# Exponentials in pairs of scales, and negated sines taken from ScalarE instead of VectorE

## The chip, the core and the metric

The kernel runs on one core of a Trainium2 chip. The time is the device time of one execution in microseconds; several executions are given with their median. The profile is of one such execution. In its rows PE is TensorE's matmuls (PEld its weight loads), DVE is VectorE, ACT is ScalarE, POOL is GpSimd and SP is SyncE, which here only issues DMAs.

## What is computed

Two independent halves, whose results are concatenated: a sliding, dilated attention (A) and a long convolution with a state-space kernel (B). Only B's kernel generation is touched by the change:

```python
def _B_ref(u, A_re, A_im, B_re, B_im, C_re, C_im, log_dt, Dskip):
    ...
    dt = jnp.exp(log_dt)[:, None]
    A = A_re + 1j * A_im
    logdA = dt * A                                   # [640, 192]
    P = jnp.exp(logdA[:, :, None] * l[None, None, :])  # l = 0 .. 2047
    K = jnp.einsum("dn,dnl,dn->dl", Cc, P, dB).real
    ...
    y = (K convolved with u along the sequence)      # by FFT of length 4096
    return y + u * Dskip[None, None, :]

return jnp.concatenate([a, b], axis=-1)
```

For each of 640 channels the kernel K has 2048 taps, each a sum over 192 complex modes of exp(l * dt * A).

## The kernel before

The 640 channels are worked off in 5 chunks of 128, `c` = 0 to 4, and each chunk in two halves, `h` = 0 and 1. A tap index is split as l = a + 8 b + 64 j, with a and b from 0 to 7 and j from 0 to 31, so that exp(l x) is a product of three factors. Each factor is a real exponential times a cosine and a sine.

*The exponentials* (`exps_chunk`, L213 to L223). `alpha` is the real part of dt * A in float32, 192 values in each partition for a chunk. The table `R` holds, for each of the 192, 48 entries: a = 0..7, then 8 b, then 64 j with j = 16..31 followed by j = 15..0. The three entries with scale 0 are set to 1 by GpSimd (L217, L218), and each of the other 45 is one ScalarE ACTIVATE, Exp with its scale, over 192 elements (L222). `R` has two buffers, R0 and R1, for even and odd chunks.

*The sines* (`trig_half`, L226 to L257). TensorE forms the phases in PSUM (`ps_ph`, L247 and L250), and ScalarE takes their sine (L255) into two tables: `TA` for a and b, and `TX` for j. `TX` has three planes of 17 entries: plane 0 (cosine, entries 0 to 16), plane 1 (sine), and plane 2, the negated sine, entries 1 to 16. For a half there are four TA operations and four TX operations on ScalarE. `TX` has one buffer, so that the sines of a half wait until the X products of the half before have read it. Exp and Sin need different ACT tables, and a table load (ACT_TABLE_LOAD) stands wherever ScalarE goes from one to the other.

*The products* (`small_half`, L268 to L296, all on VectorE). P = R's a-entries times TA, Q = P times the coefficients `cT`, F from Q; G from R's b-entries times TA; then the negated sines (L286), and for each of two quarters X = R's j-entries times TX. P has one buffer. `y_form` (L305) makes three Y products for each quarter, and `kgen_unit` multiplies X and Y on TensorE (`ps_k`, L318 and L323) to give the taps `Ksb`.

*What surrounds them.* In the same loop the FFT runs: `fwd` (matmuls at L337 and L343, their copies out of PSUM to A at L338 and to Sg at L344, both on ScalarE), products with the spectrum (L358 on VectorE), and the first stage of the inverse (L374, copy Z at L375 on ScalarE). `times_d` makes UD on VectorE (L387). ScalarE also makes two copies of the coefficients ahead of each chunk's exponentials (L206, L207).

*The order.* The program builds its instructions in the order of the code, and a scheduler puts them into one fixed queue for each engine; each engine then works strictly in its own order and waits on semaphores. `tc.issue_after(ins)` makes what follows come after `ins` on its engine, and `tc.keep_in_program_order` keeps an instruction at its place. In chunk c the code order is: products of half 0, sines of half 1, units of half 0 with transforms in between, products of half 1, then the exponentials of chunk c+1 (L748 to L750, after the last sine of half 1) and the sines of its half 0 (L751), then the units of half 1. After the fifth chunk come the attention and the second stage of the inverse FFT, which the change does not touch.

Of the kernel before, what the change touches and what calls it, by code (L numbers as in the profile page):

```python
# [10 lines left out]
A = mybir.AluOpType  # L11
ACT = mybir.ActivationFunctionType
AX = mybir.AxisListType
bf16 = mybir.dt.bfloat16
f32 = mybir.dt.float32
# [4 lines left out]
PI_LO = 3.1415925  # L20
# [31 lines left out]
    return F1, F64  # L52


R_MULT = [float(a) for a in range(8)] + [8.0 * b for b in range(8)] + [64.0 * (16 + i) for i in range(16)] + [64.0 * (31 - i) for i in range(16, 32)]
L1_OF_ROW = [16 + i for i in range(16)] + [31 - i for i in range(16, 32)]


# [23 lines left out]
def inline(nc, arr, name):  # L82
    return nc.inline_tensor(np.ascontiguousarray(arr).astype(np.float32).astype(ml_dtypes.bfloat16), name=name).ap()
# [126 lines left out]
        engine.tensor_copy(out=co[:, :, 3], in_=co[:, :, 0])  # L210


def exps_chunk(tc, pools, B, c):  # L213
    nc = tc.nc
    R = pools["tab"].tile([128, 48, NE_R, 4], bf16, name="R", tag=f"R{c % 2}")
    src = B["alpha"][:, c].rearrange("p u (q f) -> p (u q) f", f=4)
    nc.gpsimd.memset(R[:, :, 0:16:8, :], 1.0)  # L217
    nc.gpsimd.memset(R[:, :, 47, :], 1.0)  # L218
    for e, m in enumerate(R_MULT):
        if m == 0.0:  # L220
            continue
        nc.scalar.activation(out=R[:, :, e, :], in_=src, func=ACT.Exp, scale=m)  # L222
    return R  # L223


def trig_half(tc, pools, B, c, h):  # L226

    nc = tc.nc
    MM = nc.tensor.matmul
    TA = pools["tab"].tile([128, 24, 32, 4], bf16, name="TA", tag=f"TA{h}")  # L230
    TX = pools["tab"].tile([128, 24, 3, 17, 4], bf16, name="TX", tag="TX")
    CF1, CF64 = B["CF1"], B["CF64"]
    for kind in range(2):
        for uu in range(2):
            u = 2 * h + uu
            L1, L64 = B["LP"][:, 0, u, c], B["LP"][:, 1, u, c]
            qs = slice(12 * uu, 12 * uu + 12)
            if kind == 0:
                both = CF64[:, 0:1].to_broadcast([128, 16, 32])
                pair = [(TA, 0, 8, [(L1, CF1[:, 0:16]), (L64, both)]), (TA, 16, 8, [(L1, CF1[:, 16:32])])]  # L240
            else:
                pair = [(TX, 0, 9, [(L64, CF64[:, 1:19])]), (TX, 18, 8, [(L64, CF64[:, 19:35])])]
            pss = [pools["psum"].tile([128, 2, 512], f32, name="ps_ph", tag="bank2") for _ in pair]
            halves = [(ps[:, bk, 0:n * UW].rearrange("p (e w) -> p e w", w=UW), L, C[:, bk * n:bk * n + n, :], i == 0, i == len(ops) - 1)
                      for ps, (dst, e0, n, ops) in zip(pss, pair) for bk in range(2) for i, (L, C) in enumerate(ops)]
            for (o, L, rhs, first, last) in halves:
                MM(o[:, :, 0:32], lhsT=L[:, 0:128], rhs=rhs, start=first, stop=last, skip_group_check=True)  # L247
            for (o, L, rhs, first, last) in halves:
                for hh in range(2):
                    MM(o[64 * hh:64 * hh + 64, :, 32:48], lhsT=L[:, 128:192], rhs=rhs[:, :, 16 * hh:16 * hh + 16], start=False, stop=last,  # L250
                       skip_group_check=True, tile_position=(0, 64 * hh))
            for ps, (dst, e0, n, ops) in zip(pss, pair):
                words = ps[:].bitcast(mybir.dt.int16).rearrange("p b (w s) -> p b w s", s=2)[:, :, 0:n * UW, 0]
                dst = dst.rearrange("p q w e f -> p q (w e) f") if dst is TX else dst
                last = nc.scalar.activation(out=dst[:, qs, e0:e0 + 2 * n, :].rearrange("p q (b e) f -> p b e q f", b=2),  # L255
                                     in_=words.rearrange("p b (e q f) -> p b e q f", q=12, f=4), func=ACT.Sin, scale=PI_LO / 32768.0)
    return TA, TX, last  # L257


def bc(ap, axis, n):  # L260
    s = list(ap.shape)
    return ap.unsqueeze(axis).to_broadcast(s[:axis] + [n] + s[axis:])


def small_half(tc, pools, co, R4, TA, TX, h):

    nc = tc.nc
    V = nc.vector  # L268
    tab = pools["tabb"]
    R = R4[:, 24 * h:24 * h + 24]  # L270
    TT = lambda o, a, b, op: V.tensor_tensor(out=o, in0=a, in1=b, op=op)  # L271
    P = tab.tile([128, 24, 2, 8, 4], bf16, name="P", tag="P")
    F = tab.tile([128, 3, 24, 8, 4], bf16, name="F", tag="F")
    G = tab.tile([128, 4, 24, 8, 4], bf16, name="G", tag="G")
    TT(P[:], bc(R[:, :, 0:8, :], 2, 2), TA[:, :, 0:16, :].rearrange("p q (r a) f -> p q r a f", r=2), A.mult)
    Q = tab.tile([128, 24, 4, 8, 4], bf16, name="Q", tag="Y", bufs=4)
    co = co[:, 24 * h:24 * h + 24].rearrange("p q (s r) f -> p q s r f", r=2)
    TT(Q[:].rearrange("p q (s r) a f -> p q s r a f", r=2), bc(P[:], 2, 2), bc(co, 4, 8), A.mult)
    Qv = Q[:].rearrange("p q (s r) a f -> p r s q (a f)", r=2)
    TT(F[:, 1:3].rearrange("p s q a f -> p s q (a f)"), Qv[:, 0], Qv[:, 1], A.add)  # L280
    TT(F[:, 0], F[:, 1], F[:, 2], A.add)
    RB = R[:, :, 8:16, :].rearrange("p q a f -> p q (a f)")
    TT(G[:, 0:4:3].rearrange("p w q a f -> p w q (a f)"), bc(RB, 1, 2), TA[:, :, 16:32, :].rearrange("p q (w a) f -> p w q (a f)", w=2), A.mult)
    TT(G[:, 1], G[:, 3], G[:, 0], A.subtract)
    TT(G[:, 2], G[:, 3], G[:, 0], A.add)
    V.tensor_scalar(out=TX[:, :, 2, 1:17, :], in0=TX[:, :, 1, 1:17, :], scalar1=-1.0, scalar2=None, op0=A.mult)  # L286
    Xs = []
    for uu in range(2):
        qs = slice(12 * uu, 12 * uu + 12)
        X = tab.tile([128, 12, 3, 32, 4], bf16, name="X", tag="X", bufs=2)  # L290
        RX = R[:, qs, 16:48, :]
        TT(X[:, :, 0:2, 0:16, :], bc(RX[:, :, 0:16, :], 2, 2), TX[:, qs, 0:2, 0:16, :], A.mult)
        TT(X[:, :, 0:2, 16:32, :], bc(RX[:, :, 16:32, :], 2, 2), TX[:, qs, 0:3:2, 1:17, :], A.mult)
        TT(X[:, :, 2], X[:, :, 1], X[:, :, 0], A.subtract)
        Xs.append(X)
    return F, G, Xs  # L296
# [365 lines left out]
def body(tc, ctx, pools, prm, B_u, B_Dskip, Sd, Zd, UDd, A_x, A_wqkv, A_wo, out_a, out_b):  # L662
    nc = tc.nc
# [12 lines left out]
    R, trig = {}, {}  # L676
    with tc.tile_pool(name="prep_b", bufs=1) as pb, tc.tile_pool(name="prep_c", bufs=1) as pc, tc.tile_pool(name="prep_a", bufs=1) as pa, tc.tile_pool(name="psum_p", bufs=2, space=bass.MemoryType.PSUM) as psp:
        pools.update(prep_a=pa, prep_b=pb, prep_c=pc)
        B, fill = partB_prep(tc, dict(pools, psum=psp), prm)
        fill(0, 1, lambda u: None)  # L680
        Dn = pa.tile([128, 160], bf16, name="Dn")
        dsrc = B_Dskip.rearrange("(g ch) -> g ch", g=4)
        late = tc.keep_in_program_order
        late(nc.sync.dma_start(out=BD[:].rearrange("p a b n -> p (a b n)"), in_=inline(nc, cn["BD"], "c_BD")))
        late(nc.sync.dma_start(out=EA[:].rearrange("p a n -> p (a n)"), in_=inline(nc, cn["EA"], "c_EA")))
        late(nc.sync.dma_start(out=T2[:].rearrange("p a n -> p (a n)"), in_=inline(nc, cn["T2"], "c_T2")))
        for g in range(4):
            late(nc.sync.dma_start(out=Dn[32 * g:32 * g + 32, :], in_=dsrc[g].partition_broadcast(32)))
        coefficients(nc.gpsimd, B, 0)
        R[0] = exps_chunk(tc, pools, B, 0)  # L690
        trig[0, 0] = trig_half(tc, pools, B, 0, 0)
        usrc = B_u[0].rearrange("(l1 l0) (g ch) -> g l1 l0 ch", l0=64, g=4)
        fill(1, NCH, lambda g: late(nc.sync.dma_start(out=U[32 * g:32 * g + 32], in_=usrc[g])))
        nc.gpsimd.tensor_copy(out=Dsb[:], in_=Dn[:].rearrange("p (ut c) -> p c ut", c=NCH))
# [24 lines left out]
    for c in range(NCH):  # L719
# [6 lines left out]
        if c > 0:  # L726
            P1, P2, last = products(tc, pools, Sk[c - 1], Sd[c - 1], fp, True)
# [15 lines left out]
        with ExitStack() as order:  # L743
            if c > 0:
                order.enter_context(tc.issue_after(last.ins))
            F, G, Xs = small_half(tc, pools, B["cT"][:, c], R[c], *trig[c, 1][:2], 1)
        if c < LAST:
            with tc.issue_after(trig[c, 1][2].ins):  # L748
                coefficients(nc.scalar, B, c + 1)
                R[c + 1] = exps_chunk(tc, pools, B, c + 1)  # L750
            trig[c + 1, 0] = trig_half(tc, pools, B, c + 1, 0)  # L751
        else:
            att.open_q0()
# [54 lines left out]
    def fill(some, n=1):  # L808
        for f in some[0:n]:
            f()  # L810
        del some[0:n]
# [14 lines left out]
    for i0, ni, j0, nj, done in ((0, 128, 2, 3, 0), (128, 128, 2, 3, 1), (256, 128, 0, 4, None), (256, 256, 4, 1, 2), (384, 128, 0, 4, 3)):  # L826
        for w in range(W):
            att.av_step(i0, ni, j0, nj, w)
            if (done, w) in LOADS:
                qr, c = LOADS[done, w]  # L830
# [78 lines left out]
```

## Time and profile before

| | us |
|---|---|
| median of 3 executions | 439.51 |
| lowest and highest | 439.4, 442.8 |
| the profiled execution | 438.98 |
| its span, first to last instruction | 437.2 |

| group (line, engine, operation, shapes) | times | busy us | mean ns |
|---|---|---|---|
| L305 VectorE, Y, 128x3072 bf16 | 60 | 102.9 | 1751 |
| L222 ScalarE, Exp into R, 128x192 from float32 | 225 | 59.3 | 358 |
| L338 ScalarE, copy A, 128x1024 | 40 | 37.6 | 1036 |
| L344 ScalarE, copy Sg, 128x1024 | 40 | 37.6 | 1027 |
| L271 VectorE, X, 128x1536 bf16 | 40 | 36.4 | 951 |
| L255 ScalarE, Sin into TA, 128x768 | 40 | 30.6 | 822 |
| L255 ScalarE, Sin into TX, 128x864 | 20 | 18.1 | 907 |
| L255 ScalarE, Sin into TX, 128x768 | 20 | 16.5 | 826 |
| L286 VectorE, negated sines, 128x1536 bf16 | 10 | 5.5 | 554 |
| ACT_TABLE_LOAD at L222 and L255 | 9 | 11.5 | 1283 |

"Mean" is the duration of one operation from its recorded start to its end. Operations of one engine that follow each other directly overlap in the records by some 0.08 to 0.1 us, so the step from start to start is shorter than the mean, and the busy time, in which overlaps count once, is less than the count times the mean. Five chunks of 45 exponentials make the 225 at L222. A timeline row gives start, length, engine, line, operation, what it writes and reads with shapes, how many were merged into the row, and in brackets how long the engine had been idle before it and what ended that.

### The profile page before, as it was taken

Reading aid. Unit: us, or ns where it says so; the run is one execution under the profiler, and the core shown is the slowest. Engines: PE = TensorE matmul, PEld = TensorE weight load, DVE = VectorE, ACT = ScalarE, POOL = GpSimd, SP = SyncE. Lnnn points to the kernel's source line nnn. Section 1 sums busy time; section 2 is a strip of 40 time slices with the busy share of each in tenths; the row PEclk is TensorE's granted clock in tenths of the full one; section 3 lists DMA queues with packets and bytes.
Section 4 is the critical chain, followed back from the end, with each engine's and each line's share of the span. In section 5 each row is a group of like instructions: output and inputs, shape, how many; then the busy total and the mean of one; then the engine's idle time right before and its main releaser. Section 6 shows DMA issues by size and latency. Waiting matters only on the chain.

```text
span 437.2 us, 17687 instructions
## 1 busy us (share of the span) xinstructions
PE 358.4 (82%) x8041; PEld 241.1 (55%) x8041; DVE 391.3 (89%) x386; ACT 314.0 (72%) x570; POOL 44.5 (10%) x85
## 2 busy tenths in 40 slices
PE   1397659989886998879778799999899897399995
PEld 0145546866863677556665665545555674134443
DVE  7889999999997999999999989946978989999751
ACT  3974998889999899979997845342858344544663
POOL 7440000000000000000010000400001204102110
PEclk9996577999999898889999899999999999659999
DMA  5569102163233402324079933500210907957343
GB/s 143 186 141 200 18 3 109 39 227 94 99 123 123 97 28 98 144 103 99 27 258 241 236 75 135 178 0 3 67 32 1 265 17 201 228 141 225 96 107 114
DMA packets 45131, 51.62 MB, mean 118 GB/s; under 512 B 31376, under 2 KB 38992, under 8 KB 42368
## 3 DMA queue, kind: packets, MB, share of 16 engines
q1 hardware_dynamic: 41520, 41.41, 35.4%
q0 software_dynamic: 3392, 8.95, 7.0%
q8 instruction: 63, 1.03, 1.0%
q10 hardware_dynamic: 144, 0.12, 0.1%
q14 instruction: 12, 0.10, 0.1%
HBM read 28.03 MB, written 18.35 MB: 106 GB/s over the span
## 4 chain that ended last, share of the span: by engine, by line
PE 49%; ACT 29%; DVE 14%; issue 5%; DMA 1%; SPq 1%; DVEq 0%; ACTq 0%
ACT R L222 10%; ACT A L338 6%; PE ps_k L318 6%; PE ps_ph L247 6%; PE ps_k L323 6%; PE ps_op L420 6%; PE ps_k L470 4%; PE ps_q L488 4%; PE ps_ph L250 4%; ACT Sg L344 4%; PE ps_f L343 4%; PE ps_v L501 2%; DVE prod L521 2%; ACT Z L375 2%; PE ps_o L420 2%
## 5 line engine op out<-in xcount | busy, mean ns | idle before, releaser
L305 DVE TENSOR_TENSOR Y<-F,G 128x3072 bf16<-128x3072 bf16 x60 | 102.9, 1751 | 0.6 <-PE ps_k L323 0.6
L222 ACT ACTIVATE R<-LPC 128x192 bf16<-128x192 f32 x225 | 59.3, 358 | 0.1
L247 PE MATMUL ps_ph<-LPC 128*128 128x256 bf16 (+1 forms) x200 | 41.5, 311 | 17.3 <-DMA LPC<-lo 8.7
L318 PE MATMUL ps_k<-Y,X 128*32 128x64 bf16 x1920 | 47.2, 239 | 7.3 <-DVE Y L305 3.8
L323 PE MATMUL ps_k<-Y,X 64*32 64x64 bf16 x1920 | 43.8, 233 | 3.4 <-issue 3.3
L344 ACT CAST Sg<-ps_f 128x1024 bf16<-128x1024 f32 x40 | 37.6, 1027 | 7.3 <-PE ps_f L343 7.3
L318 PEld LDWEIGHTS <-X 128*32 128x32 bf16 x1920 | 32.1, 117 | 17.4 <-issue 9.0
L343 PE MATMUL ps_f<-A,T 128*128 128x128 bf16 x320 | 27.3, 259 | 14.9 <-ACT A L338 14.2
L338 ACT CAST A<-ps_f 128x1024 bf16<-128x1024 f32 x40 | 37.6, 1036 | 0.7 <-PE ps_f L337 0.6
L271 DVE TENSOR_TENSOR X<-R,TX 128x1536 bf16<-128x1536 bf16 x40 | 36.4, 951 | 0.0
L323 PEld LDWEIGHTS <-X 64*32 64x32 bf16 x1920 | 29.6, 113 | 12.1 <-issue 4.4
L255 ACT ACTIVATE TX<-ps_ph 128x864 bf16<-128x864 int16 (+1 forms) x40 | 31.9, 867 | 5.3 <-DVE X L271 2.5
L343 PEld LDWEIGHTS <-T 128*128 128x128 bf16 x320 | 25.6, 119 | 16.1 <-issue 14.9
L585 DVE TENSOR_TENSOR prod<-v,atp 128x2048 bf16<-128x2048 bf16 (+2 forms) x32 | 31.3, 1018 | 2.0 <-PE ps_o L420 1.8
L255 ACT ACTIVATE TA<-ps_ph 128x768 bf16<-128x768 int16 x40 | 30.6, 822 | 3.4 <-PE ps_ph L250 3.0
L250 PE MATMUL ps_ph<-LPC 128*64 128x128 bf16 (+1 forms) x400 | 29.6, 249 | 0.0
L247 PEld LDWEIGHTS <-LPC 128*128 128x128 bf16 x200 | 15.0, 102 | 25.9 <-issue 19.1
L420 PE MATMUL ps_op<-wo,o 128*128 128x320 bf16 x160 | 28.5, 315 | 0.8 <-ACT o L595 0.4
L358 DVE TENSOR_TENSOR P<-P,Sg 128x4096 bf16<-128x4096 bf16 x10 | 22.9, 2288 | 4.1 <-DMA P<-Sdram 3.2
L250 PEld LDWEIGHTS <-LPC 128*64 128x64 bf16 x400 | 15.2, 118 | 19.1 <-issue 18.9
L611 ACT CAST ob<-ps_op 128x320 bf16<-128x320 f32 x28 | 11.9, 431 | 19.0 <-PE ps_op L420 17.3
L337 PE MATMUL ps_f<-BD,U 128*64 128x128 bf16 x320 | 19.4, 285 | 6.1 <-ACT A L338 3.3
(129 smaller groups left out, 661.2 us busy)
## 6 DMA issues: line engine op xcount, KB each, us to landing
Sdram<-Sg SPq DMA_DIRECT2D x5, 1024.0 KB
P<-Sdram SPq DMA_DIRECT2D x5, 1024.0 KB
P<-Sdram SPq DMA_DIRECT2D x10, 512.0 KB
Zdram<-Z SPq DMA_DIRECT2D x5, 1024.0 KB
Z<-Zdram SPq DMA_DIRECT2D x30, 128.0 KB
U<-in_B_u_dram SPq DMA_DIRECT2D x4, 640.0 KB
UDdram<-UD SPq DMA_DIRECT2D x10, 256.0 KB
out_dram<-ysb SPq DMA_DIRECT2D x32, 80.0 KB
```

The costliest lines, as they stand in the source:

```text
L222: nc.scalar.activation(out=R[:, :, e, :], in_=src, func=ACT.Exp, scale=m)
L247: MM(o[:, :, 0:32], lhsT=L[:, 0:128], rhs=rhs, start=first, stop=last, skip_group_check=True)
L250: MM(o[64 * hh:64 * hh + 64, :, 32:48], lhsT=L[:, 128:192], rhs=rhs[:, :, 16 * hh:16 * hh + 16], start=False, stop=last, skip_group_check= ...
L255: last = nc.scalar.activation(out=dst[:, qs, e0:e0 + 2 * n, :].rearrange("p q (b e) f -> p b e q f", b=2), in_=words.rearrange("p b (e q f ...
L271: TT = lambda o, a, b, op: V.tensor_tensor(out=o, in0=a, in1=b, op=op)
L305: nc.vector.tensor_tensor(out=Y[:].rearrange("p q (b a) f -> p q b a f", a=8), in0=fa, in1=gb, op=A.mult)
L318: MM(ps[32 * g:32 * g + 32, t], lhsT=X[:, q, 2 - k, :, f], rhs=Ys[k][:, q, :, f], start=(t == 0 and k == 0), stop=False, tile_position=(0, ...
L323: MM(ps[32 * g:32 * g + 32, t], lhsT=X[hb, q, 2 - k, :, f], rhs=Ys[k][hb, q, :, f], start=False, stop=(k == 2), tile_position=(64 * (g // ...
L338: nc.scalar.copy(out=A1[:, :, 32 * b:32 * b + 32].rearrange("p k (j g) -> p k j g", g=4), in_=ps[:].rearrange("p j k g -> p k j g"))
L343: last = MM(ps[:, kk], lhsT=C["T2"][:, 8 * b + kk, :], rhs=A1[:, 8 * b + kk, :], start=(kk % 4 == 0), stop=True, skip_group_check=True)
L344: nc.scalar.copy(out=Sg[:, :, 8 * b:8 * b + 8, :], in_=ps[:].rearrange("p k (j g) -> p j k g", g=4))
L420: self.MM = lambda *a, **k: self.tc.keep_in_program_order(self.nc.tensor.matmul(*a, **k))
```

## The change

The scale-0 entries are still set by GpSimd. For the others, `exps_chunk` first makes a tile `twice` with two planes, 2 * alpha and alpha, in float32. Entries whose scales are m and 2 m are then written by one ACTIVATE on 384 elements, which reads both planes with scale m and writes both entries; entries that have no partner are written as before, from alpha. For the scales 1 to 7 these are the pairs (1, 2) and (3, 6) and the single entries 4, 5, 7; the same for 8 to 56; for 64 j there are 10 pairs and 11 single entries. In all there are 17 single operations and 14 pairs in a chunk, and the single ones come first in the code.

The two planes are made on VectorE for chunk 0, in a tile of their own, and on GpSimd for chunks 1 to 4, where `twice` takes the buffer of P (`tag="P"`).

In `trig_half` each PSUM tile with the sines of j is read by a second Sin with the negated scale, which writes plane 2 of TX; the VectorE operation at L286 goes.

```diff
-R_MULT = [float(a) for a in range(8)] + ...
...
-def exps_chunk(tc, pools, B, c):
+def exps_chunk(tc, pools, B, c, engine, twice):
     nc = tc.nc
     R = pools["tab"].tile([128, 48, NE_R, 4], bf16, name="R", tag=f"R{c % 2}")
-    src = B["alpha"][:, c].rearrange("p u (q f) -> p (u q) f", f=4)
+    alpha = B["alpha"][:, c].rearrange("p u w -> p (u w)")
+    for b in range(2):
+        engine.tensor_scalar(out=twice[:, b], in0=alpha, scalar1=2.0 - b, scalar2=None, op0=A.mult)
     nc.gpsimd.memset(R[:, :, 0:16:8, :], 1.0)
     nc.gpsimd.memset(R[:, :, 47, :], 1.0)
-    for e, m in enumerate(R_MULT):
-        if m == 0.0:
-            continue
-        nc.scalar.activation(out=R[:, :, e, :], in_=src, func=ACT.Exp, scale=m)
+    one, two = [], []
+    for places in ({a: a for a in range(1, 8)}, {8 * a: 8 + a for a in range(1, 8)}, {64 * j: j if j > 15 else 47 - j for j in range(1, 32)}):
+        left = sorted(places)
+        while left:
+            m = left.pop(0)
+            e, step = places[m], 0
+            if 2 * m in left:
+                left.remove(2 * m)
+                step = places[2 * m] - e
+            (two if step else one).append((m, e, step))
+    for m, e, step in one + two:
+        src = twice[:].rearrange("p b (q f) -> p q b f", f=4)
+        if step == 0:
+            src, out = alpha.rearrange("p (q f) -> p q f", f=4), R[:, :, e, :]
+        elif step < 0:
+            out = R[:, :, e + step:e + 1:-step, :]
+        else:
+            src, out = src[:, :, ::-1, :], R[:, :, e:e + step + 1:step, :]
+        nc.scalar.activation(out=out, in_=src, func=ACT.Exp, scale=float(m))
     return R
...
-                last = nc.scalar.activation(out=dst[:, qs, e0:e0 + 2 * n, :]..., func=ACT.Sin, scale=PI_LO / 32768.0)
+                for at, sign in ((e0, 1), (35, -1))[:2 if e0 == 18 else 1]:
+                    last = nc.scalar.activation(out=dst[:, qs, at:at + 2 * n, :]..., func=ACT.Sin, scale=sign * PI_LO / 32768.0)
...
-    V.tensor_scalar(out=TX[:, :, 2, 1:17, :], in0=TX[:, :, 1, 1:17, :], scalar1=-1.0, scalar2=None, op0=A.mult)
...
-        R[0] = exps_chunk(tc, pools, B, 0)
+        R[0] = exps_chunk(tc, pools, B, 0, nc.vector, pa.tile([128, 2, 192], f32, name="twice"))
...
         if c < LAST:
+            twice = pools["tabb"].tile([128, 2, 192], f32, name="twice", tag="P")
             with tc.issue_after(trig[c, 1][2].ins):
                 coefficients(nc.scalar, B, c + 1)
-                R[c + 1] = exps_chunk(tc, pools, B, c + 1)
+                R[c + 1] = exps_chunk(tc, pools, B, c + 1, nc.gpsimd, twice)
```

More of the change, by code (lines that the diff above doesn't have):

```diff
@@ L52, in table_consts_np @@
     return F1, F64
-R_MULT = [float(a) for a in range(8)] + [8.0 * b for b in range(8)] + [64.0 * (16 + i) for i in range(16)] + [64.0 * (31 - i) for i in range(16, 32)]
 L1_OF_ROW = [16 + i for i in range(16)] + [31 - i for i in range(16, 32)]
@@ L254, in trig_half @@
                 dst = dst.rearrange("p q w e f -> p q (w e) f") if dst is TX else dst
-                last = nc.scalar.activation(out=dst[:, qs, e0:e0 + 2 * n, :].rearrange("p q (b e) f -> p b e q f", b=2),
-                                     in_=words.rearrange("p b (e q f) -> p b e q f", q=12, f=4), func=ACT.Sin, scale=PI_LO / 32768.0)
+                for at, sign in ((e0, 1), (35, -1))[:2 if e0 == 18 else 1]:
+                    last = nc.scalar.activation(out=dst[:, qs, at:at + 2 * n, :].rearrange("p q (b e) f -> p b e q f", b=2),
+                                         in_=words.rearrange("p b (e q f) -> p b e q f", q=12, f=4), func=ACT.Sin, scale=sign * PI_LO / 32768.0)
     return TA, TX, last
```

## The prediction

> **What bounds the kernel now.** I read the page's busy times first, then the chain of waits, the timelines of the three engines that the edits touch, and a table of VectorE's busy time by stretch.
>
> ```profile
> PE 358.4 (82%) x8041; PEld 241.1 (55%) x8041; DVE 391.3 (89%) x386; ACT 314.0 (72%) x570; POOL 44.5 (10%) x85
> PE 49%; ACT 29%; DVE 14%; issue 5%; DMA 1%; SPq 1%; DVEq 0%; ACTq 0%
> ```
>
> VectorE (DVE in the rows) is busiest and ScalarE (ACT) takes 29% of the chain, but these are means over stages. The edits lie in the stage up to 285 us, so I asked for VectorE's busy time in four stretches of it (start:end, length, busy, operations): in each chunk from shortly before product P of half 1 to the same product of the next chunk's half 0.
>
> ```profile
> core 0: us, DVE busy (x), PEclk, DMA share, GB/s
> 54.00:76.00 22.00, 22.00 (x22) 0.77 0.11 45
> 106.00:133.00 27.00, 24.33 (x23) 0.94 0.29 105
> 160.00:184.00 24.00, 24.00 (x23) 0.91 0.29 113
> 211.00:234.00 23.00, 23.00 (x23) 0.93 0.60 194
> ```
>
> Three of the four have no idle time at all; each operation starts some 0.08 us before the one ahead of it ends. The idle 2.7 us of the second lie at its end:
>
> ```profile
> 131.04 3.16 ACT L255 ACTIVATE TA<-ps_ph 128x768 bf16<-128x768 int16 x4
> ...
> 133.35 0.96 DVE L271 TENSOR_TENSOR P<-R,TA 128x1536 bf16<-128x1536 bf16 x1 [3.02 <-ACT TA L255]
> ...
> 184.28 0.95 DVE L271 TENSOR_TENSOR P<-R,TA 128x1536 bf16<-128x1536 bf16 x1
> ```
>
> P(2,0), product P of chunk 2's half 0, waited 3.02 us for its sines. At 184.28 they had been there for about 1 us, at 233.99 for 0.7. VectorE sets the pace, and ScalarE's queue of exponentials, table load and sines comes in just ahead of it.
>
> **VectorE's side.** Ten negations go (TX at L286, 554 ns, 0.47 from start to start). Nine lie in the dense stretch: 9 x 0.47 = 4.2 us off it. The tenth, at 30.80, had itself waited 1.29 us for ScalarE.
>
> **ScalarE's sines.** Twenty are added, on 128x768. The four TA sines at 231.04 take 2.92 us: (2.92 - 0.81) / 3 = 0.70 each from start to start; the mean row of the TX sines, 826 ns, is the upper bound. I take 0.71, so 2.84 us a chunk.
>
> **ScalarE's exponentials.** The 45 of a chunk become 17 single ones and 14 pairs, the same elements in fewer starts. A single one costs 11.49 us / 45 = 0.255. A pair has 192 elements more; the 480- and 320-wide copies to ysb (563 and 429 ns) give 0.84 ns an element, so 0.255 + 0.16 = 0.415. That saves 0.09 a pair, 1.3 us a chunk. Bounds: nothing (two singles, 0.51) and 3.6 (a pair as dear as a single). Net, ScalarE gains 1.5 us of work a chunk. In the first chunk the 1.3 us are on the path: the sines wait for the exponentials that run from 9.79 to 21.30, while the first TA matmuls are done by 20.8. Two copies of alpha on VectorE there (0.17 each by the like row at L177) sit before a 1.69 us wait of VectorE and cost nothing; without that cover, 0.35.
>
> **The copies on GpSimd.** For chunks 1 to 4 GpSimd makes two copies of alpha, one doubled, into `twice`, which takes the buffer of P. They wait for Q(c,1), the last reader of P: done at 58.2, 109.8, 163.8 and 214.7. All 14 pairs of the next chunk wait for them, and ScalarE works in order: behind a waiting pair stand the remaining pairs, the table load, the TA sines of P(c+1,0), and whatever copies out of PSUM were put after it. On GpSimd's queue stand the memsets of R and later the loads of wkq, all with tens of us to spare. So the question is when GpSimd (POOL) gets to run. These are the rows of GpSimd operations that read SBUF beside VectorE, with VectorE's own:
>
> ```profile
> 25.15 1.80 POOL L209 TENSOR_SCALAR cT<-cT 128x192 bf16<-128x192 bf16 x1 [0.54 <-ACT cT L196]
> ...
> 279.80 3.98 POOL L481 COPY kT<-kT 128x280 bf16<-128x280 bf16 x1 [5.74 <-ACT kT L471]
> ```
>
> ```profile
> 25.44 0.95 DVE L191 TENSOR_TENSOR p<-p,p 128x768 f32<-128x768 f32 x1
> 26.42 1.18 DVE L193 TENSOR_SCALAR cn<-p,dtc 128x192 bf16<-128x192 f32 x4
> ...
> 276.74 6.75 DVE L305 TENSOR_TENSOR Y<-F,G 128x3072 bf16<-128x3072 bf16 x4
> 286.48 1.30 DVE L518 TENSOR_TENSOR prod<-ql,kT 128x1024 bf16<-128x1024 bf16 x2 [2.99 <-ACT ql L489]
> ```
>
> The kT copy starts at 279.80 and ends at 283.78. VectorE's run of Y products ends at 276.74 + 6.75 = 283.49: the copy ends 0.29 us after VectorE falls idle, having let two starts of a Y pass. The operation at L209 spans one start of a TENSOR_TENSOR and ends at 26.94, 0.55 us after the last of them (26.39). Another GpSimd copy of 192 elements, beside TENSOR_SCALARs, took 0.34. I read this as GpSimd shut out while VectorE runs TENSOR_TENSORs without a gap. From Q(c,1) to P(c+1,0) there is nothing else on VectorE once the negation is gone.
>
> The Trainium skill ("SBUF — State Buffer", Who interferes with whom) says that a VectorE operation with two SBUF inputs and a GpSimd operation that reads SBUF exclude each other, and that whoever issues first holds the ports for one whole instruction. By that, GpSimd waits out one VectorE operation, 1.75 us at most; the kT copy waited out three, and the row decides. The skill's "Perfetto Trace Analysis" (GPSIMD Engine Instruction) calls reported GpSimd spans unreliable, which is a reason for not being surer of this than I am.
>
> **The sum.** With GpSimd shut out, `twice` is written only when VectorE has nothing left to start, which is at P(c+1,0) itself. From there: two copies at 0.29 to 0.55, say 0.85 together; 14 pairs at 0.415, 5.8; table load 1.28; three sines, 2 x 0.71 + 0.81 = 2.2. That is 10.1 us of VectorE standing still in each of four chunks. It replaces waits of 0.57 (at 76.67, behind P(1,0)), 3.02, 0 and 0: 9.5 + 7.1 + 10.1 + 10.1 = 36.8. Off this go 4.2 for the negations, 1.3 at the start, and about 1 of the two waits at 250.4 and 255.3 (0.92 and 1.17), as TensorE and the loads have had time. Net +30.3. On the profiled execution, 438.98 us (span 437.2, the rest around it), that is 469.3; the median shown, 439.51, is 0.5 above it: **470 us**.
>
> Its own bounds: if a pair stands ahead of the four Sg copies, ScalarE has 3.7 us more to do after release (13.8 a chunk, about +45: 485). But TensorE then stops too for want of PSUM, and VectorE may run out of Y buffers and stop up to 4.6 us early, which lets GpSimd in sooner; with the Sg copies ahead that leaves 5.5 a chunk (+12: 452).
>
> **Rivals.**
>
> *GpSimd gets in promptly* (the other side). Then `twice` is there some 3 us after Q(c,1), while the 17 single exponentials still cover ScalarE for 4.3. The place that decides is the sines of P(c+1,0): ScalarE's period of 50.5 us (180.50 to 231.04) grows by 1.5, VectorE's of 49.7 (184.28 to 233.99) shrinks by 0.9, less two GpSimd copies that now block it. P(2,0) comes out +0.4 (two exponential batches at -1.3, three sets of added sines at +1.42, start -1.3); two chunks more add 3.0, of which some 2 us vanish in ScalarE's present waits (5 us in those 100) and 0.7 in the lead of the sines. The last half gives back 0.5: 438.98 + 0.2 + 0.5, about **440**. For it: two spans are thin evidence. Against: both rows say otherwise. The rule of the Trainium skill weighed above, taken by itself, gives this rival.
>
> *VectorE stays the bound and ScalarE keeps up*: -4.2 - 1.3 = -5.5, so **434**. For it: VectorE's dense stretch. Against: the sines' lead of under 1 us, and the copies' own time on the shared ports.
>
> *The copies out of PSUM queue behind the pairs as well*: Z (2.8 for three), A (3.7), a TensorE reply (1.1) and Sg (3.7) after release, 11.3 more, less the 4.6 that VectorE stops early: +6.7 in four chunks, **497**. For it: in the profile the exponentials stand ahead of A at 57 to 61. Against: from chunk 1 on most A and Z stand ahead of the last exponentials.
>
> That the change does not do what it says is no rival of weight: each pair is one ACTIVATE with 384 elements.
>
> **Chances and range.** GpSimd shut out with the order as now 0.63; the same with copies behind the pairs 0.11; prompt 0.19; VectorE bound 0.07. About 1%, 4.4 us, is what a measurement here can tell from no change. The first two are slower by more than that (0.74), the third within it (0.19), the fourth faster (0.07). The forecast's own range is 452 to 486; down to 438 it takes in the prompt rival and leaves out 0.07 below and 0.11 above.
>
> **What would show it.** Right: the GpSimd TENSOR_SCALARs on `twice` have long spans that end within 0.6 us of the end of a VectorE run; ScalarE idle before a pair, released by GpSimd; P(c+1,0) waiting 5 to 14 us for TA in four chunks; 384-wide exponentials near 0.41 from start to start. Wrong: those spans under 2 us, with VectorE's operations stretched instead; no ScalarE wait on GpSimd; then the time is near 440 and the sines' lead decides. If pairs cost 0.5 each, a chunk gains 1.3 us.

## The result, and the profile after

| | before | after |
|---|---|---|
| median of 6 executions, us | 440.19 | 492.37 |
| lowest and highest | 438.2, 442.8 | 486.1, 496.4 |
| the profiled execution, us | 438.98 | 486.13 |
| its span | 437.2 | 484.4 |

The changed kernel takes 1.1137 times as long, 95% interval 1.1053 to 1.122. Ratios here and below leave out executions that lie over 1.5% above the fastest of their kernel (here 495.8 and 496.4 us), while medians keep them. By the medians it is 52 us more, where 30 were forecast, and the median lies 6 us above the range.

From the page of the changed kernel, first the busy times, then the chain by engine, then three of its costliest groups (busy us and mean ns of one, then idle time ahead and what ended most of it):

```profile
PE 363.0 (75%) x8041; PEld 242.2 (50%) x8041; DVE 389.4 (80%) x378; ACT 321.6 (66%) x520; POOL 97.7 (20%) x93
...
PE 27%; DVE 8%; ACT 7%; issue 3%; ACTq 0%; DVEq 0%
...
L323 DVE TENSOR_TENSOR Y<-F,G 128x3072 bf16<-128x3072 bf16 x60 | 103.3, 1754 | 31.3 <-PE ps_k L341 31.3
L219 POOL TENSOR_SCALAR twice<-LPC 128x192 f32<-128x192 f32 x8 | 55.6, 6965 | 168.7 <-DVE Q L290 103.1
...
L240 ACT ACTIVATE R<-twice 128x384 bf16<-128x384 f32 x70 | 29.6, 516 | 37.5 <-POOL twice L219 37.5
```

No engine has much more work than before (VectorE even 2 us less); the span is longer because engines stand still. GpSimd (POOL) is the exception: its eight copies into `twice` show 55.6 us, 7.0 us each, and ScalarE waits 37.5 us for them. The chain is of less use here: its shares add up to 45% only, and GpSimd does not appear in it.

The table of VectorE's busy time (start:end, length, busy, operations), for the stretches that answer to the four shown of before:

```profile
core 0: us, DVE busy (x), PEclk, DMA share, GB/s
55.40:95.90 40.50, 21.65 (x21) 0.66 0.09 34
131.70:157.30 25.60, 24.63 (x23) 0.93 0.27 106
182.90:218.10 35.20, 24.45 (x24) 0.78 0.30 114
243.80:278.00 34.20, 23.22 (x22) 0.80 0.49 147
```

The three stretches that had no gap before now hold 18.9 us of idle time (chunk 0), 10.8 (chunk 2) and 11.0 (chunk 3); that of chunk 1, which had 2.7, holds only 1.0. GpSimd's timeline says why:

```profile
59.24 16.40 POOL L219 TENSOR_SCALAR twice<-LPC 128x192 f32<-128x192 f32 x2 [26.33 <-issue]
135.32 1.86 POOL L219 TENSOR_SCALAR twice<-LPC 128x192 f32<-128x192 f32 x2 [59.12 <-DVE Q L290]
186.69 20.98 POOL L219 TENSOR_SCALAR twice<-LPC 128x192 f32<-128x192 f32 x2 [43.96 <-DVE Q L290]
247.57 16.38 POOL L219 TENSOR_SCALAR twice<-LPC 128x192 f32<-128x192 f32 x2 [39.34 <-ACT R L240]
```

and VectorE's timeline at the end of the third:

```profile
205.16 1.30 DVE L405 TENSOR_TENSOR UD<-U,Dsb 128x1024 bf16<-128x1024 bf16 x1
217.22 0.96 DVE L290 TENSOR_TENSOR P<-R,TA 128x1536 bf16<-128x1536 bf16 x1 [10.75 <-ACT TA L274]
```

Of the 20.98 us, 20.32 are the first of the two copies (the longest in its group). It ends at 186.69 + 20.32 = 207.01, 0.55 us after VectorE's last operation ended at 206.46; the second takes the rest. The first copies of chunks 0 and 3 end 0.55 us after VectorE's run as well. Then ScalarE does the 14 pairs, the table load and the sines while VectorE stands at P(3,0) for 10.75 us.

Chunk 0 costs more, and ScalarE's timeline shows why:

```profile
75.68 5.89 ACT L240 ACTIVATE R<-twice 128x384 bf16<-128x384 f32 x14 [18.05 <-POOL twice L219]
81.47 3.72 ACT L356 CAST A<-ps_f 128x1024 bf16<-128x1024 f32 x4
86.29 3.76 ACT L362 CAST Sg<-ps_f 128x1024 bf16<-128x1024 f32 x4 [1.10 <-PE ps_f L361]
90.07 1.28 ACT L274 ACT_TABLE_LOAD   x1
91.36 2.23 ACT L274 ACTIVATE TA<-ps_ph 128x768 bf16<-128x768 int16 x3
```

with TensorE's timeline

```profile
82.51 1.19 PE L355 MATMUL ps_f<-BD,U 128*64 128x128 bf16 x16 [22.70 <-ACT A L356]
```

and VectorE's:

```profile
72.69 1.75 DVE L323 TENSOR_TENSOR Y<-F,G 128x3072 bf16<-128x3072 bf16 x1
93.28 1.76 DVE L323 TENSOR_TENSOR Y<-F,G 128x3072 bf16<-128x3072 bf16 x1 [18.85 <-PE ps_k L341]
```

Four copies A and four copies Sg stand behind the 14 pairs. TensorE waits 22.7 us for A to empty PSUM, with the taps' matmuls behind in its queue; these alone free the Y buffers, so VectorE runs out of buffers with Y products still to make. That stop lets the copies in, but ScalarE then has 15.7 us of its queue to work through (75.68 to 91.36) before the first sine.

By stretch, between the starts of the products P(c,0), in us of change against before. "Forecast" takes the terms of the sum in their places, with 0.47 off for each of the nine negations (one lies in the stretch from P(0,0), two in each later one); "second profile" is of run e8 below, the same kernel once more:

| stretch | forecast | after | second profile |
|---|---|---|---|
| start to P(0,0), at 33.87 before | -1.3 | +0.8 | +0.6 |
| P(0,0) to P(1,0), 41.9 before | +9.1 | +18.4 | +18.3 |
| P(1,0) to P(2,0), 57.6 | +6.1 | +3.8 | +12.6 |
| P(2,0) to P(3,0), 50.9 | +9.2 | +9.9 | +10.8 |
| P(3,0) to P(4,0), 49.7 | +9.2 | +10.2 | +10.3 |
| P(4,0) to the last Y, 49.5 | -1.9 | +2.7 | +3.0 |
| after that, 153.7 | 0 | +1.4 | +1.4 |
| sum | +30.4 | +47.2 | +57.0 |

The second profile lies 26.6 us above the forecast: 9.2 in the stretch from P(0,0), 6.5 in that from P(1,0), 4.9 in the last one before the attention, 6.0 in the others together. No cause was found for the 1.4 us behind the last Y.

### The profile page after: what moved, and what is told of

Same layout as the page of the kernel before. It is cut to its first block, busy times and chain, and to the rows that moved or that the text cites. A ratio compares the mean times of both kernels' runs of the same rounds, so it can differ in the third digit from the quotient of the medians.

```text
span 484.4 us, 17644 instructions
## 1 busy us (share of the span) xinstructions
PE 363.0 (75%) x8041; PEld 242.2 (50%) x8041; DVE 389.4 (80%) x378; ACT 321.6 (66%) x520; POOL 97.7 (20%) x93
## 5 line engine op out<-in xcount | busy, mean ns | idle before, releaser
L219 POOL TENSOR_SCALAR twice<-LPC 128x192 f32<-128x192 f32 x8 | 55.6, 6965 | 168.7 <-DVE Q L290 103.1
L265 PE MATMUL ps_ph<-LPC 128*128 128x256 bf16 (+1 forms) x200 | 43.0, 320 | 30.9 <-ACT TA L274 11.8
L240 ACT ACTIVATE R<-twice 128x384 bf16<-128x384 f32 x70 | 29.6, 516 | 37.5 <-POOL twice L219 37.5
L274 ACT ACTIVATE TX<-ps_ph 128x768 bf16<-128x768 int16 (+1 forms) x60 | 45.6, 862 | 8.2 <-DVE X L290 5.5
L355 PE MATMUL ps_f<-BD,U 128*64 128x128 bf16 x320 | 19.9, 280 | 23.6 <-ACT A L356 22.7
L341 PEld LDWEIGHTS <-X 64*32 64x32 bf16 x1920 | 29.8, 113 | 10.8 <-issue 2.7
L355 PEld LDWEIGHTS <-U 128*64 128x64 bf16 x320 | 19.1, 206 | 24.3 <-issue 23.5
L376 DVE TENSOR_TENSOR P<-P,Sg 128x4096 bf16<-128x4096 bf16 x10 | 22.8, 2285 | 8.6 <-DMA P<-Sdram 8.4
```

Of the source, the lines that this page charges most:

```text
L219: engine.tensor_scalar(out=twice[:, b], in0=alpha, scalar1=2.0 - b, scalar2=None, op0=A.mult)
L274: last = nc.scalar.activation(out=dst[:, qs, at:at + 2 * n, :].rearrange("p q (b e) f -> p b e q f", b=2), in_=words.rearrange("p b (e q f ...
L341: MM(ps[32 * g:32 * g + 32, t], lhsT=X[hb, q, 2 - k, :, f], rhs=Ys[k][hb, q, :, f], start=False, stop=(k == 2), tile_position=(64 * (g // ...
L355: MM(ps[64 * ri:64 * ri + 64, j], lhsT=src_fn(8 * b + j), rhs=C["BD"][:, wh, ri, :], start=(j % 4 == 0), stop=True, skip_group_check=True, ...
```

## The experiments

The theory, called ports theory in the expectations: GpSimd's copies are shut out by VectorE's two-input operations, and all else follows from ScalarE's fixed order behind the late pairs. The rivals: the copies are late because they wait for the buffer of P, whatever engine makes them (buffer theory); the added sines and the longer exponentials are too much for ScalarE (load theory); GpSimd itself is slow. Ratios are to the kernel before, run on the same chip beside each.

**e1, the copies on VectorE.**

```diff
-                R[c + 1] = exps_chunk(tc, pools, B, c + 1, nc.gpsimd, twice)
+                R[c + 1] = exps_chunk(tc, pools, B, c + 1, nc.vector, twice)
```

> The two copies of alpha of chunks 1 to 4 are made by VectorE in place of GpSimd; all else is the changed kernel. Ports theory (GpSimd's copies are shut out while VectorE runs two-input operations without a gap, and ScalarE stands in order behind the pairs that wait for them): the copies take 0.25 us each at their place in VectorE's queue, ScalarE waits under 1 us for them in each chunk, and the time falls from 492 to about 441 us (438 to 446). Buffer theory (the copies come late because they wait for the buffer of P, whatever engine makes them): ScalarE still waits 10 us or more in three chunks, 480 or more. Load theory (the added sines and the longer exponentials are what ScalarE can't fit in): 480 or more, with no wait on the copies.

452.03 us, ratio 1.0166 (1.0093 to 1.0239). With 0.26 us a copy, 9.7 of the 11.4 points are gone by this one word. The rest was not expected. ScalarE's timeline:

```profile
67.71 1.35 ACT L240 ACTIVATE R<-twice 128x384 bf16<-128x384 f32 x3 [9.31 <-DVE twice L219]
```

In chunk 0 the scheduler put the two copies at 66.38 and 67.42 in VectorE's queue, among the X products, so that ScalarE's queue stood for 9.3 us even so. That stretch is 8.3 us longer than before, P(1,0) to P(2,0) is 3.1 longer, and the start costs 1.6.

**e2, the second sines alone, in the kernel before.**

```diff
-                last = nc.scalar.activation(out=dst[:, qs, e0:e0 + 2 * n, :]..., func=ACT.Sin, scale=PI_LO / 32768.0)
+                for at, sign in ((e0, 1), (35, -1))[:2 if e0 == 18 else 1]:
+                    last = nc.scalar.activation(out=dst[:, qs, at:at + 2 * n, :]..., func=ACT.Sin, scale=sign * PI_LO / 32768.0)
...
-    V.tensor_scalar(out=TX[:, :, 2, 1:17, :], in0=TX[:, :, 1, 1:17, :], scalar1=-1.0, scalar2=None, op0=A.mult)
```

> The kernel before with the second sine on ScalarE in place of VectorE's negation; the exponentials stay single, there are no copies. Ports theory: ScalarE has 2.8 us a chunk more, VectorE 0.9 us less; ScalarE's lead in front of P(c+1,0) was under 1 us, so some of it shows: 445 us (439 to 451). Load theory: most of the 52 us of the change is here, 470 or more. Buffer theory: as the ports theory.

446.81 us, ratio 1.0099 (1.0054 to 1.0143). Three products P(c+1,0) wait 3.79, 2.57 and 2.82 us for their sines, 9.2 in all where before had one wait of 3.02. VectorE loses its negations and waits longer than it saved: in these places ScalarE, not VectorE, sets the pace once the sines are added to it.

**e3, the pairs alone** (the changed kernel with VectorE's negation back and no second sine).

```diff
-                for at, sign in ((e0, 1), (35, -1))[:2 if e0 == 18 else 1]:
+                for at, sign in ((e0, 1), (35, -1))[:1]:
...
+    V.tensor_scalar(out=TX[:, :, 2, 1:17, :], in0=TX[:, :, 1, 1:17, :], scalar1=-1.0, scalar2=None, op0=A.mult)
```

> The changed kernel with VectorE's negation put back and the second sine taken out; the pairs and GpSimd's copies stay. Ports theory: the waits of ScalarE on GpSimd's copies stay (8 to 20 us in three or four chunks), 488 us (478 to 500). Load theory: ScalarE has less to do than in the kernel before, so 436 to 440.

490.33 us, ratio 1.1028 (1.0967 to 1.109). The pairs bring 10.3% by themselves, e2's sines 1.0%; together they give the 11.4%. All four sets of copies are late here (16.9, 21.5, 16.9 and 16.9 us). VectorE's row holds the negation again, and it does not let GpSimd in either; in chunk 0, where the first copy waits from 60.39 to 76.60:

```profile
62.41 0.56 DVE L305 TENSOR_SCALAR TX<-TX 128x1536 bf16<-128x1536 bf16 x1
```

This operation reads one input only. So the row that shuts GpSimd out need not be of two-input operations alone.

**e4, only the copies on GpSimd, and nobody reads them** (added to the kernel before, in the same place and the same buffer).

```diff
+            idle = pools["tabb"].tile([128, 2, 192], f32, name="idle", tag="P")
+            for b in range(2):
+                nc.gpsimd.tensor_scalar(out=idle[:, b], in0=B["alpha"][:, c + 1]..., scalar1=2.0 - b, scalar2=None, op0=A.mult)
```

> The kernel before with two GpSimd copies of alpha added in each of chunks 0 to 3, written into the buffer of P after Q(c,1) and read by nobody. Ports theory: the first copy of a chunk shows a span of 10 to 20 us that ends within 0.6 us of the end of a VectorE run in most chunks; ScalarE doesn't wait for it, only P(c+1,0) does, for the buffer, 1 to 2 us a chunk: 445 us (441 to 449). Buffer theory: the copies take under 2 us once Q is done, and the time is that of the kernel before.

446.22 us, ratio 1.004 (1.0004 to 1.0077). From the timelines of GpSimd and VectorE, in that order:

```profile
166.41 21.52 POOL L750 TENSOR_SCALAR idle<-LPC 128x192 f32<-128x192 f32 x2 [32.19 <-DVE Q L271]
```

```profile
185.43 1.32 DVE L387 TENSOR_TENSOR UD<-U,Dsb 128x1024 bf16<-128x1024 bf16 x1
187.97 0.96 DVE L271 TENSOR_TENSOR P<-R,TA 128x1536 bf16<-128x1536 bf16 x1 [1.23 <-POOL idle L750]
```

The spans are there (18.6, 21.5, 21.5 and 20.3 us) with no pair in the kernel. They are not GpSimd's speed: they end when VectorE has nothing left to start, and VectorE then waits 1.2 us for the buffer of P. So late copies are nearly free by themselves; what is dear is who waits for them.

**e5, four short VectorE operations that read nothing,** put into the products of half 1 (they clear a part of Q that nothing reads any more).

```diff
+    pause = lambda: V.memset(Q[:, 0:3], 0.0) if h == 1 else None
+    pause()
     TT(F[:, 0], F[:, 1], F[:, 2], A.add)
+    pause()
...
         TT(X[:, :, 0:2, 0:16, :], bc(RX[:, :, 0:16, :], 2, 2), TX[:, qs, 0:2, 0:16, :], A.mult)
+        pause()
```

> The changed kernel with four short VectorE memsets added in each half 1, behind the operations that follow Q(c,1): operations that read nothing from SBUF, into the dead Q. Ports theory: GpSimd's read gets in during one of them; the copies on GpSimd span under 4 us in each chunk, ScalarE waits under 3 us for them, and the time is near that of the changed kernel with copies that aren't late, 452 us (444 to 462). If GpSimd is shut out by a busy VectorE whatever it runs, the spans stay at 15 to 21 us and the time at 488 or more.

452.13 us, ratio 1.0177 (1.0071 to 1.0283). GpSimd's timeline:

```profile
119.02 2.83 POOL L219 TENSOR_SCALAR twice<-LPC 128x192 f32<-128x192 f32 x2 [52.01 <-DVE Q L290]
```

and VectorE's:

```profile
120.63 0.22 DVE L300 MEMSET Q<- 128x192 uint32 x1
120.77 0.49 DVE L290 TENSOR_TENSOR F<-F 128x768 bf16<-128x768 bf16 x1
```

All four sets of copies take 2.83 to 2.85 us. The first copy takes 2.17 of them and ends at 121.19, 0.34 us behind the first of the memsets. GpSimd does the same work as in the changed kernel, and VectorE more than there; opening VectorE's row with memsets of 0.22 us gives back nearly all the loss. (In chunk 0 ScalarE still waits 4.5 us for the copies, more than the 3 expected.) This settles the mechanism: it is the unbroken row of operations that read SBUF that shuts GpSimd out, and not a busy VectorE as such. Which property of the memset lets GpSimd in, that it reads nothing or that it is short, was not separated.

**e6, one pair behind 43 single exponentials** (the kernel before with the copies and only the scales 960 and 1920 as a pair).

```diff
-        if m == 0.0:
+        if m == 0.0 or twice is not None and e in (30, 32):
...
+    if twice is not None:
+        for b in range(2):
+            nc.gpsimd.tensor_scalar(out=twice[:, b], in0=..., scalar1=2.0 - b, scalar2=None, op0=A.mult)
+        nc.scalar.activation(out=R[:, :, 30:33:2, :], in_=twice[:]..., func=ACT.Exp, scale=960.0)
```

> The kernel before with GpSimd's two copies in chunks 0 to 3 and one single pair for each of the next chunks, placed behind the 43 single exponentials; VectorE's negation stays. Ports theory: ScalarE waits for the copies as long as in the changed kernel, but behind the release stand only that pair, the table load, the sines and what the scheduler puts behind the pair: 0.85 + 0.45 + 1.28 + 2.2 = 4.8 us at P(c+1,0) instead of 10.1, four times less the waits that were there (3.6), so 459 us (452 to 470). Load theory: 441 to 444, since ScalarE has less to do than before.

473.64 us, ratio 1.0557 (1.0434 to 1.0681): a single waiting instruction for each chunk costs over half of what fourteen cost in e3. In three chunks P(c+1,0) waits 5.38, 5.39 and 5.40 us, where the sum without 13 pairs gives 10.1 - 13 x 0.415 = 4.7. The rest lies in chunk 0, where A and Sg stand behind the one pair, as behind the fourteen, and VectorE waits 13.0 us for TensorE, and in an X product after P(4,0) that waits 8.8 us for TensorE. The execution profiled took 480.5 us, the longest of the four, so its waits do not account for the median; for the 8.8 us in particular the profile shows no cause (TensorE stands 10.2 us there without waiting for anything that is shown), and the other executions have no profile.

**e7, the pairs kept behind the last Sg copy** (all else as changed).

```diff
+        with ExitStack() as order:
+            if step and behind is not None:
+                order.enter_context(tc.issue_after(behind))
+            nc.scalar.activation(out=out, in_=src, func=ACT.Exp, scale=float(m))
...
-                R[c + 1] = exps_chunk(tc, pools, B, c + 1, nc.gpsimd, twice)
+                R[c + 1] = exps_chunk(tc, pools, B, c + 1, nc.gpsimd, twice, C["sg"].ins)
```

> The changed kernel with the pairs of a chunk ordered behind the last Sg copy ahead of them on ScalarE, so that no copy out of PSUM waits behind a pair that waits for GpSimd. Ports theory: the copies on GpSimd are as late as before, but each chunk costs the 10 us of the prediction's sum and not 15 to 19 as in chunks 0 and 3: about 475 us (468 to 482). If the order behind the pairs doesn't matter, 492 as the changed kernel.

476.68 us, ratio 1.0708 (1.0638 to 1.0778). VectorE's timeline in chunk 0, to set beside the 18.85 above:

```profile
78.61 1.31 DVE L408 TENSOR_TENSOR UD<-U,Dsb 128x1024 bf16<-128x1024 bf16 x1
90.69 0.96 DVE L293 TENSOR_TENSOR P<-R,TA 128x1536 bf16<-128x1536 bf16 x1 [10.77 <-ACT TA L277]
```

Chunks 2 and 3 wait 10.76 and 10.77. In chunk 1 the copies got in early again (1.85 us), as in the first profile of the changed kernel, and P(2,0) waits 3.2. With A and Sg ahead of the pairs, VectorE finishes its row, and the stall is the forecast's: pairs, table load, three sines.

**e8, the changed kernel once more,** for a second profile.

> The changed kernel once more, for a second profile: in the first, GpSimd got in promptly in chunk 1 (1.9 us for both copies) and that execution was 5 to 7 us below the others. Ports theory: a profile of an execution near 492 shows four late first copies and a wait at P(2,0) of 5 to 11 us.

495.99 us, close to the longest of the first six. Now the copies of chunk 1 are late too (20.98 us), and P(2,0) waits 10.76 for its sines. The two profiled executions differ by 9.9 us, and the stretch from P(1,0) to P(2,0) by 8.8 of them.

**e9 and e10, the copies of chunks 1 to 4 on ScalarE itself,** with the second sines (e9) and with VectorE's negation in their place (e10, by the two lines of e3).

```diff
+        if engine is nc.scalar:
+            engine.activation(out=twice[:, b], in_=alpha, func=ACT.Copy, scale=2.0 - b)
+        else:
             engine.tensor_scalar(out=twice[:, b], in0=alpha, scalar1=2.0 - b, scalar2=None, op0=A.mult)
...
-                R[c + 1] = exps_chunk(tc, pools, B, c + 1, nc.gpsimd, twice)
+                R[c + 1] = exps_chunk(tc, pools, B, c + 1, nc.scalar, twice)
```

> The changed kernel with the copies of chunks 1 to 4 made by ScalarE itself, in front of the pairs, in place of GpSimd. Ports theory: no wait on another engine is left but that for Q(c,1), some 2 us in chunk 0; ScalarE has 0.5 us a chunk more. With the second sines that leaves it a little behind VectorE: 447 us (442 to 453). Buffer theory: 470 or more.

> As the run with ScalarE's own copies, with VectorE's negation back and without the second sines: pairs alone, and no GpSimd. ScalarE has 1.3 - 0.5 = 0.8 us a chunk less than in the kernel before, VectorE the same. Ports theory: about the time of the kernel before, ratio 0.995 to 1.005; it would be the version to beat the kernel before if ScalarE's lead in front of P(c+1,0) is worth anything.

e9: 448.15 us, ratio 1.0147 (1.0073 to 1.022). e10: 445.81, ratio 1.0102 (1.0062 to 1.0142). The copies then wait for no other engine but in chunk 0 (1.5 us, for Q(0,1)), so this is about what the rest of the change is worth, with 0.5 us of copies a chunk on ScalarE: still a loss. e10 should have been level with before, and was not. VectorE's timeline near the start, where chunk 0's copies are still VectorE's:

```profile
10.49 0.26 DVE L222 TENSOR_SCALAR twice<-LPC 128x192 f32<-128x192 f32 x1 [2.06 <-ACT LPC L154]
```

The copy waits 2.06 us for alpha, and the operations that form the phases stand behind it. P(0,0) starts at 35.2, 1.3 later than before; the forecast had it 1.3 earlier.

**e11, pairs in chunk 0 alone, copies on ScalarE, and e12, pairs in all chunks, all copies on ScalarE** (both with VectorE's negation). e12 against e10:

```diff
-        R[0] = exps_chunk(tc, pools, B, 0, nc.vector, pa.tile([128, 2, 192], f32, name="twice"))
+        R[0] = exps_chunk(tc, pools, B, 0, nc.scalar, pa.tile([128, 2, 192], f32, name="twice"))
```

In e11, besides, chunks 1 to 4 write every entry from alpha by its own ACTIVATE, as before:

```diff
-                R[c + 1] = exps_chunk(tc, pools, B, c + 1, nc.scalar, twice)
+                R[c + 1] = exps_chunk(tc, pools, B, c + 1, nc.scalar, None)
```

> The kernel before with pairs in chunk 0 alone, whose two copies of alpha ScalarE makes itself; chunks 1 to 4 keep single exponentials and VectorE's negation. If the start of the changed kernel lost its gain because VectorE's copies waited in order for alpha and held back the phases, the phases here come as early as in the kernel before, the 45 exponentials take 10.2 + 0.5 us instead of 11.5, and the first product P starts up to 0.8 us earlier: ratio 0.996 to 1.002. If not, P(0,0) starts at 34.2 or later again.

> Pairs in all chunks with ScalarE's own copies in all five, VectorE's negation as before: the run with negation and ScalarE's copies, without VectorE's two copies in chunk 0. If these held back the start, P(0,0) starts at 33 to 34 instead of 35.2 and the time falls by about 1.3 us, to a ratio of 1.005 to 1.009 over the kernel before; what is left is ScalarE's wait for Q(0,1) in chunk 0.

e11: 440.06 us, ratio 0.9988 (0.9958 to 1.0018), no difference that can be measured. e12: 442.66, ratio 1.0049 (1.0017 to 1.0081). In e12 P(0,0) starts at 32.76, 1.1 us ahead of before and 2.45 ahead of e10; in e11, whose start is built the same way, at 33.58, only 0.3 ahead of before. In the eight profiles with the two copies on VectorE it starts at 34.5 to 35.8, in the four without pairs in chunk 0 at 33.8 to 34.2. So the copies on VectorE cost some 2 us, and without them the pairs bring the start forward by 0.3 to 1.1. In e12 that gain is not kept: P(1,0) comes at 76.61, 0.9 later than before. No version tried beats the kernel before.

## Why the prediction was right in its direction and too small

**GpSimd shut out, right.** In all 22 late cases (after, e3, e4, e6, e7, e8) the first copy ends 0.53 to 0.55 us after VectorE's row, and e4 and e5 show the cause by adding the copies alone and by opening the row. The Trainium skill ("SBUF — State Buffer", Who interferes with whom) has the exclusion, and the trace agrees with it, chunk 1 of two profiles apart (last section); but its holding of the ports for one whole instruction is not what was seen, since the copy of 20.3 us saw 17 operations start, each of 1.8 us at most. That nothing else is on VectorE "once the negation is gone" did not matter: with the negation in the row (e3, e4) the copies were as late. The rival of prompt copies falls with it, and even with copies that aren't late (e5, e9) the kernel is not level with before, as that rival had it, but 1.8% and 1.5% slower.

**The stall in a chunk, right in kind and near in size.** 10.1 us were forecast, and 10.75 to 10.77 measured wherever the copies were late and nothing but pairs, table load and sines stood behind the wait (after, e7, e8). The pair costs 0.41 from start to start (5.89 us for 14), as forecast.

**The order of ScalarE's queue, wrong: the step that failed.** The sum took "the order as now" to mean that nothing but pairs, table load and sines stands behind the wait, and gave the case with copies out of PSUM behind the pairs a chance of 0.11 and a price of 6.7 us in each of four chunks. But the order of before already is that case in chunk 0. ScalarE's timeline there:

```profile
57.25 4.16 ACT L222 ACTIVATE R<-LPC 128x192 bf16<-128x192 f32 x16
61.31 3.72 ACT L338 CAST A<-ps_f 128x1024 bf16<-128x1024 f32 x4
66.13 3.76 ACT L344 CAST Sg<-ps_f 128x1024 bf16<-128x1024 f32 x4 [1.10 <-PE ps_f L343]
```

All exponentials stand ahead of A and Sg. The forecast read this ("at 57 to 61") and used it only for the rival; there the stretch grew by 18.4 in place of 9.1. In chunk 3 of the changed kernel two pairs stand ahead of the four Sg:

```profile
263.98 0.94 ACT L240 ACTIVATE R<-twice 128x384 bf16<-128x384 f32 x2 [9.44 <-POOL twice L219]
264.82 3.73 ACT L362 CAST Sg<-ps_f 128x1024 bf16<-128x1024 f32 x4
268.43 5.09 ACT L240 ACTIVATE R<-twice 128x384 bf16<-128x384 f32 x12
```

VectorE waits 9.42 us for TensorE there, then 1.56 at P(4,0) and 3.69 behind it, and the last stretch gained 2.7 in place of losing 1.9. So the rival came true in two chunks of four. Nor did VectorE's early stop give back 4.6 in chunk 0: it ran out of buffers one Y product (1.7 us) ahead of P(1,0). With the order mended, e7 comes to 8.7 us less in profiles where chunk 1 is alike (475.7 against 484.4); between the medians it is 15.7, and the ratio falls by 4.3 points.

**Chunk 1's wait for the spectrum, missed.** A product at L376 waits 5.5 us in chunk 1 for the load of the spectrum, which the sum does not have. That the late Sg of chunk 0 delays this load was not tried, and cannot be all: in e2 and e9, where that Sg is not held up by GpSimd, the same product waits 2.9 and 3.3 us for it. In the second profile it waits 4.9, which the profile puts down to ScalarE's sines. With the copies late too (10.76, in place of the 3.02 of before) these make most of the +12.6, where 6.1 were forecast.

**The copies in chunk 0 that "cost nothing", wrong.** Counted was the wait behind them as cover; but they themselves wait for alpha (2 us) in an in-order queue, ahead of work that was ready. They cost some 2 us (e10 to e12), so the start lost 0.8 where 1.3 were to be gained.

**The sines, half right.** Their time (0.70 from start to start) was as forecast. The sum let them vanish; e2 puts the trade of sines for negations at +1.0%, 4 us, and e9 over e10 at about 0.4%, where the intervals overlap. Negations gone: VectorE's busy time in the chunks falls by 3.3 us (243.9 to 240.6) where 4.2 were forecast.

**The range.** Its upper end was one bound (a pair ahead of Sg) and left out the case above. The execution that was profiled (486.1) came near that end because chunk 1's copies got in early, which is luck.

## What to carry to other kernels

Before an operation is given to an idle engine, ask what on the other engines can shut it out: a GpSimd copy of 0.7 us took 20 here, because VectorE had no gap for it. Price a wait by what stands behind the waiting instruction in its engine's queue, place by place in every chunk: one pair cost about half of what fourteen did. An operation put early in an in-order queue costs its own wait, even if something behind it waits later anyway.

## What the hardware showed that was not expected

GpSimd sometimes got in without a gap. VectorE's timeline of the changed kernel, chunk 1, where its copies start at 135.32:

```profile
135.06 0.55 DVE L290 TENSOR_TENSOR G<-G 128x768 bf16<-128x768 bf16 x1
135.53 1.10 DVE L290 TENSOR_TENSOR F<-Q 128x1536 bf16<-128x1536 bf16 x1
136.54 0.69 DVE L290 TENSOR_TENSOR G<-G 128x768 bf16<-128x768 bf16 x1
```

F takes 1.10 us and G 0.69, where they take 0.95 and 0.55 elsewhere, while the two copies take 0.84 and 1.05 where 0.68 is the least: both engines ran side by side, each somewhat slower. It happened in chunk 1 of two profiles (after, e7), not in that of e3 and e8, and in no other chunk of these. What decides it was not found; that it accounts for the spread of the changed kernel's executions, 486 to 496 us, fits the two profiled ones and was not tried on others.
